# Turning weights in place between two chains, instead of turning, storing and loading them back

## The chip, the cores, the metric

One core of one Trainium2 chip. The metric is the device time of one execution in microseconds (us), as a median of several.

The chain of the kernel works in order of time, so most readings are lengths of stages, from one landmark to the next. Six batches of runs were made, and the kernel before has medians from 3148 to 3178 us over them. Every run is therefore compared with the runs of the kernel before in its own batch.

## The reference, cut to what matters

A memory-augmented recurrent attention over 64 segments of 32 rows, with 8 memory rows in front, 32 heads of 128, model width 512; and beside it a dense layer with squared ReLU. Asked for are the output and all gradients.

```python
mem = mem0
for s in range(n_seg):                                  # 64 steps, each needs mem of the last
    h = jnp.concatenate([mem, xs[s]], axis=1)           # 8 + 32 rows of 512
    q, k, v = (jnp.einsum('btd,dhe->bhte', h, W) for W in (Wq, Wk, Wv))
    p = _softmax(jnp.where(mask, jnp.einsum('bhqe,bhke->bhqk', q, k) * scale, -1e9))
    o = jnp.einsum('bhte,hed->btd', jnp.einsum('bhqk,bhke->bhqe', p, v), Wo)
    mem = o[:, :M, :].copy()
# out = x + A(layernorm(x)) + B(layernorm(x)); returned: out and the vjp with grad_out
```

The backward pass needs each weight with its two inner axes exchanged ("turned"): the forward projections contract over the model width, the backward ones over the head's columns.

## The kernel before: the parts that the argument touches

PE is TensorE, DVE VectorE, ACT ScalarE, POOL GpSimd; PEld are TensorE's weight loads, SPq is the Sync queue. Names that begin with S_ are tensors in DRAM. vM holds the values of a block's memory rows, loaded back from S_A, into which f_N, the projections of a step, are stored. dN are the projections of the rows that do not feed the recurrence (the left rows); OT, OC and OCl are attention outputs on their way to DRAM, OTL and ON those of the left rows; gol is their incoming gradient. A gather is a product with Wo (in the backward chain with another turned weight) that brings the heads back to the model width. The seam is the stretch between the last forward projection and the first product of the left rows. A weight is 4 MB in bf16. The forward chain plays 16 blocks of 4 steps in a fixed order for each engine. In each step the kernel turned 128 x 1024 elements: eight transposes on PE (`wt`), a copy from PSUM to SBUF on DVE (`we`), a store of 256 KB on the Sync queue (`ws`):

```python
def wt():
    ps["wt"] = fr.tile([P, 8 * P], BF16, name="ps_wt", tag="r")
    for n in range(8):
        ...                                             # x = a 128 x 128 block of Wo, Wv, Wk or Wq
        transpose_to(ps["wt"][:, n * P:(n + 1) * P], x)
def we():
    st["wt"] = fo.tile([P, 8 * P], BF16, name="wtt", tag="wtt")      # one buffer
    ENGS["we"](st["wt"][:], ps["wt"][:])
def ws():
    dma(S_WOT[...] if t == 3 else S_WT[...], st["wt"][:]...)         # Sync queue
# ... and the eviction of other rows shares that buffer:
    st["dN", i // 2] = fo.tile([P, GW], BF16, name="dN", tag="wtt")
```

At the end of the chain a load on the GpSimd queue brings turned Wo back to where Wq and Wk were; the others come in twelve loads of 1 MB, one in each iteration of the next stage (the "left rows": the work of the backward pass that doesn't depend on the recurrence, mixed with products for the dense layer's weight gradients, which read `wA` and `wB`):

```python
def load_back():
    wq_cm.__exit__(None, None, None); wk_cm.__exit__(None, None, None)
    ...
    back["WoT"] = bw.tile([P, DC, HD], BF16, name="WoT")
    pdma(back["WoT"][:], S_WOT[:])
# left rows:
def chunk(b, eng=dma):
    ...
    side[b > 0] = wg.tile([P, TC, D], BF16, name="wA", tag="wA", bufs=1)
    eng(side[b > 0][:], ...)                            # wA, 2 MB
    part[b] = wg.tile([P, TC, CH], BF16, name="wB", tag="wB")
    eng(part[b][:], ...)                                # wB, 1 MB
o["first"] = lambda: (load(i_, nc.scalar), chunk(i_, pdma))
...
    for t, h in pieces[i_:i_ + 1]:
        pdma(WT[t][:, h:h + 8, :], S_WT[:, t, h:h + 8, :])
```

## Time and profile before

| | us |
|---|---|
| median of the first three runs | 3175.75 (3164.9 to 3184.37) |
| profiled span | 3166.7 |
| forward chain, first to last forward projection | 917.2 |
| from there to the last left gather of the forward pass | 30.6 |
| from there to the first product of the left rows (wA, wB) | 52.7 |
| left rows, from there to the first backward projection | 228.9 |
| backward chain, first to last backward projection | 963.6 |

A row of groups gives busy time and mean duration; a wait gives its total, how often, and the longest; a timeline row gives start, duration and in brackets the idle time before it and what ended it.

### The profile page before, as it was taken

The page shows a single profiled execution, that of the slowest core. Times are in us where ns is not written, and L with a number is a line of the kernel's source. Part 1 is how long each engine was busy: PE and PEld are TensorE (multiplying, and loading weights), DVE is VectorE, ACT ScalarE, POOL GpSimd, SP SyncE. Part 2 cuts the span into 40 slices and gives each one's busy share as a digit, 9 for nine tenths or more (in the row PEclk, how much of TensorE's full clock was granted, in tenths as well). Part 3 has the DMA queues.
Part 4 walks back from the last instruction along what each step waited for, and adds up shares of the span by engine and source line. Part 5 has one row for each costly group of instructions (what it writes and reads, how often), then busy time and mean ns, then how long its engine had stood idle before and what let it go on. Part 6 is the DMA issues. An engine that isn't in the chain of part 4 may idle for free.

```text
span 3166.7 us, 115555 instructions
## 1 busy us (share of the span) xinstructions
PE 2726.4 (86%) x51672; PEld 1404.3 (44%) x51672; DVE 1261.0 (40%) x3515; ACT 1012.6 (32%) x2356; POOL 384.3 (12%) x702
## 2 busy tenths in 40 slices
PE   8996899999999885478789888888888649999998
PEld 4453455555554442235444444444444324444443
DVE  5442555555565563232444444444444301100101
ACT  2322444444454442122333333333333201111111
POOL 0000000000000000122222222222222100000000
PEclk9998999999999997789999999999999879999999
DMA  9557476666767767999577677767766799999993
GB/s 265 163 183 210 123 196 186 183 181 190 190 170 191 181 175 196 233 290 263 142 185 173 162 188 172 170 172 183 172 162 188 176 229 193 220 184 217 183 186 85
DMA packets 842563, 594.40 MB, mean 188 GB/s; under 512 B 595745, under 2 KB 726578, under 8 KB 837074
## 3 DMA queue, kind: packets, MB, share of 16 engines
q1 hardware_dynamic: 814850, 489.73, 65.0%
q0 software_dynamic: 25584, 96.10, 9.8%
q8 instruction: 405, 6.64, 0.9%
q10 hardware_dynamic: 1632, 1.18, 0.1%
q14 instruction: 92, 0.75, 0.1%
HBM read 205.14 MB, written 250.10 MB: 144 GB/s over the span
## 4 chain that ended last, share of the span: by engine, by line
PE 29%; SPq 9%; ACT 4%; DMA 3%; issue 3%; DVE 2%; ACTq 0%; POOLq 0%; POOL 0%; DVEq 0%
PE ps_gR L431 9%; PE ps_gw L1471 8%; SPq L1396 6%; PE b_pp L518 4%; PE ps_proj L390 3%; DMA out_dram<-wt 2%; PE ps_RL L1168 2%; PE ps_sum L440 2%; ACT gk L374 1%; ACT gON L374 1%; ACT gv L374 1%; SPq L1382 1%; DMA gn<-S_ON 1%; ACT R L374 1%; SPq L1399 1%
## 5 line engine op out<-in xcount | busy, mean ns | idle before, releaser
L1471 PE MATMUL ps_gw<-gn,HNc 128*128 128x512 bf16 x1920 | 418.5, 380 | 8.5 <-ACT wt L1446 8.5
L1471 PEld LDWEIGHTS <-HNc 128*128 128x128 bf16 x1920 | 188.3, 98 | 234.1 <-issue 11.5
L374 ACT CAST f_N<-ps_proj 128x512 bf16<-128x512 f32 x384 | 218.1, 587 | 193.5 <-PE ps_proj L390 155.5
L1446 ACT CAST wt<-ps_gw 128x512 bf16<-128x512 f32 x126 | 69.2, 592 | 560.3 <-DMA out_dram<-wt 361.6
L390 PEld LDWEIGHTS <-X 128*32 128x32 bf16 x6144 | 160.3, 99 | 175.8 <-issue 22.7
L1429 DVE TENSOR_TENSOR gx<-ps_rows,gb 128x512 f32<-128x512 f32 x16 | 11.1, 692 | 423.0 <-PE ps_rows L1427 392.4
L1471 PE MATMUL ps_gw<-GOc,gn 128*128 128x512 bf16 x640 | 142.6, 386 | 28.1 <-DMA gn<-S_ON 28.1
L431 PE MATMUL ps_gR<-WT,gv 128*32 128x512 bf16 x2048 | 150.8, 388 | 11.3 <-ACT gOT L374 4.2
L431 PE MATMUL ps_gR<-WT,gk 128*32 128x512 bf16 x2048 | 142.4, 395 | 9.8 <-ACT gk L374 6.6
L390 PE MATMUL ps_proj<-Wk,X 128*32 128x512 bf16 x2048 | 137.9, 403 | 8.2 <-DVE X L915 4.0
L431 PE MATMUL ps_gR<-WT,gq 128*32 128x512 bf16 x2048 | 140.4, 397 | 3.9 <-issue 3.9
L390 PE MATMUL ps_proj<-Wq,X 128*32 128x512 bf16 x2048 | 134.5, 394 | 6.6 <-DVE X L453 6.5
L374 ACT CAST gON<-ps_proj 128x512 bf16<-128x512 f32 x128 | 75.0, 586 | 165.5 <-PE ps_proj L390 160.2
L390 PE MATMUL ps_proj<-WoT,GT 128*32 128x512 bf16 x2048 | 123.6, 383 | 4.5 <-POOL GT L1198 3.3
L829 POOL COPY kM<-f_kT 128x256 bf16<-128x256 bf16 x64 | 25.8, 402 | 831.9 <-DVE f_kT L377 831.9
L431 PE MATMUL ps_R<-Wo,OT 128*32 128x512 bf16 x2048 | 122.6, 380 | 1.2 <-DVE OT L377 1.2
L440 PE MATMUL ps_sum<-identF,R 128*128 128x128 f32 x512 | 102.1, 300 | 25.0 <-ACT R L374 16.1
L390 PE MATMUL ps_proj<-Wv,X 128*32 128x512 bf16 x2048 | 121.6, 378 | 0.0
L1471 PEld LDWEIGHTS <-gn 128*128 128x128 bf16 x640 | 63.5, 99 | 105.9 <-DMA gn<-S_ON 28.4
L374 ACT CAST gk<-b_pp 128x256 bf16<-128x256 f32 x192 | 65.9, 381 | 138.7 <-PE b_pp L518 132.3
L440 PEld LDWEIGHTS ps_sum<-identF,R 128*128 128x128 f32 x512 | 56.9, 145 | 86.3 <-ACT R L374 58.9
L377 DVE COPY R<-ps_gR 128x256 f32<-128x256 f32 x64 | 27.2, 425 | 157.6 <-ACT R L374 116.0
(241 smaller groups left out, 4886.4 us busy)
## 6 DMA issues: line engine op xcount, KB each, us to landing
S_A<-f_N SPq DMA_DIRECT2D x64, 512.0 KB
S_A<-f_N SPq DMA_DIRECT2D x64, 256.0 KB
S_GB<-gv SPq DMA_DIRECT2D x32, 512.0 KB
S_GB<-gq SPq DMA_DIRECT2D x32, 512.0 KB
S_GB<-gk SPq DMA_DIRECT2D x32, 512.0 KB
gn<-S_ON SPq DMA_DIRECT2D x16, 1024.0 KB
out_dram<-wt SPq DMA_DIRECT2D x128, 128.0 KB
b_kN<-S_A POOLq DMA_DIRECT2D x63, 256.0 KB, 4.1
```

What stands on the lines that cost most here:

```text
L374: nc.scalar.copy(out, in_)
L377: nc.vector.tensor_copy(out, in_)
L390: nc.tensor.matmul(ps[32 * g:32 * g + 32, :], lhsT=hT[:, dc, :], rhs=W[:, dc, c:c + 4 * P], start=(dc == 0), stop=(dc == DC - 1), tile_pos ...
L431: nc.tensor.matmul(R[32 * g:32 * g + 32, :], lhsT=XT(k, g), rhs=W[:, g * KH + k, :], start=(first and k == 4 * h), stop=(last and k == 4 * ...
L440: nc.tensor.transpose(st["T"][:, c * P:(c + 1) * P], R4()[:, c * P:(c + 1) * P], identF[:])
L518: nc.tensor.matmul(o, lhsT=N_[32 * g:32 * g + m, kk * P:(kk + 1) * P], rhs=X(kk)[32 * g:32 * g + m], start=(i == 0), stop=(i == len(jobs) ...
L1168: nc.tensor.matmul(ps["R", i][32 * g:32 * g + 32, :], lhsT=B_[n][:, k, g, :], rhs=W[:, g * KH + k, :], start=(ps["n", i] == 1 and m == 0), ...
L1382: nc.sync.dma_start_transpose(t_[:, 0:NB, dc * P:(dc + 1) * P], srcT[:, dc, :])
L1396: nc.sync.dma_start_transpose(t_[:, b, :].rearrange("p (k e) -> p k e", k=KH), blocks(b)[:, g].rearrange("p k r -> p (k r)"))
L1399: dma(t_[32 * j:32 * j + 32, NB:RC_ALL, :], left_(g).rearrange("(c j) r x -> j r c x", j=SPB)[j])
L1446: nc.any.tensor_copy(wt[:], ps[:])
L1471: nc.tensor.matmul(ps[:], lhsT=l(rc), rhs=r(rc), start=(n == 0), stop=(n == RC_ALL - 1))
```

## The change

Intent: the weights have the same size turned as unturned, so each 128 x 1024 block can be turned where it lies: eight transposes into PSUM and one copy back over the block. Nothing is stored or loaded, and no turning runs inside the forward chain: 18 turns of Wk and Wq and 16 of Wo run in its tail, 30 more (the rest of Wq, and Wv) in the iterations of the left rows. The price: turned in place, a weight is read as four runs of 128 columns with gaps.

```diff
-    S_WT = dram.tile([P, 3, H, D], BF16, name="S_WT")
-    S_WOT = dram.tile([P, DC, HD], BF16, name="S_WOT")
...
+    def turned_columns(W):
+        return lambda dc, c: W[:, c // P:c // P + 4, dc * P:(dc + 1) * P]
+    def turned_heads(W):
+        return lambda h: W[:, :, h * P:(h + 1) * P]
+    def turn_weight(ps, W, n, ev):
+        x = W[:].rearrange("p a b -> p (a b)")[:, n * 8 * P:(n + 1) * 8 * P]
+        for i in range(8):
+            transpose_to(ps[:, i * P:(i + 1) * P], x[:, i * P:(i + 1) * P])
+        ev(x, ps[:])
... (weight_turn with wt, we, ws, and all their places in the order: removed)
-            pdma(back["WoT"][:], S_WOT[:])
+        TURNS = [(Wqkv[t], n) for t in (1, 0, 2) for n in range(HD * DC // (8 * P))]
+        TURNS_O = [(Wo, n) for n in range(HD * DC // (8 * P))]
+            after = {"ob0": 2, "ob1": 2, "L.tu1": 10, "L.ob1": 2, "L.G1": 1, "L.G0": 1}
+            after_o = {"L.ra": 6, "L.tb": 5, "L.xt": 5}
... (left rows:)
-                for t, h in pieces[i_:i_ + 1]:
-                    pdma(WT[t][:, h:h + 8, :], S_WT[:, t, h:h + 8, :])
+                def T_(i=i):
+                    if TURNS:
+                        turn_weight(lr.tile([P, 8 * P], BF16, name="ps_wt", tag="r"), *TURNS.pop(0), (acp, vcp)[i])
... (projections and gathers read through columns, heads_of, turned_columns, turned_heads;
     the buffers of the left rows are laid out anew, as the weights keep their places)
```

## The prediction

> **What bounds the kernel now.** I read the busy slices of the page first, then the busy times by stage, then the waits, then the order of time at the seams. The stages are known from which tiles run when: forward chain 308 to 1215 us, its tail to 1253, start of the left-rows stage to 1303, that stage to 1532, backward chain to 2512, weight gradients to the end.
>
> ```profile
> PE   8996899999999885478789888888888649999998
> ...
> DMA  9557476666767767999577677767766799999993
> ...
> 308.00:1215.00 907.00, 838.63 (x18799) 450.33 (x18800) 531.90 (x1567) 422.49 (x934) 51.23 (x127) 0.98 0.66 178
> ...
> 1253.00:1303.00 50.00, 4.40 (x108) 2.42 (x108) 4.96 (x12) 2.15 (x4) 2.66 (x5) 0.55 0.96 212
> 1303.00:1532.00 229.00, 175.07 (x3276) 106.53 (x3278) 71.55 (x166) 59.56 (x138) 52.84 (x100) 0.92 0.96 257
> ```
>
> The columns of a stage are PE, PEld, DVE, ACT and POOL busy, granted clock, DMA share, GB/s. The forward chain has PE busy 838.6 of 907 us (92%) and the DMA engines 66%: PE and the recurrence bound it. From 1253 to 1532 it is the reverse: DMA share 0.96, PE idle 45.6 of 50 and 53.9 of 229 us. That is where DMA traffic has a price.
>
> In the forward chain I looked for what the turning costs there. Its PE part is small (eight transposes at 57 ns from start to start, 0.45 us a step), its DVE copy 0.68 us a step:
>
> ```profile
> L165 PE MATMUL ps_wt<-ident,Wv x128: 219/219/230, 530.4 to 743.5; 128*128 128x128 bf16 x128
> L377 DVE COPY wtt<-ps_wt x64: 651/682/693, 312.8 to 1207.4; 128x1024 bf16<-128x1024 bf16 x64
> ...
> SPq L796 <- DVE wtt L377: 85.3, 35, 7.0
> ...
> PE f_pp L518 <- DMA vM<-S_A: 21.2, 28, 1.5
> ...
> 998.14 0.40 SPq L899 DMA_DIRECT2D S_A<-E  x1
> 1002.04 0.32 SPq L796 DMA_DIRECT2D S_WT<-wtt  x1
> 1002.41 1.33 SPq L678 DMA_TRANSPOSE OC<-OT  x1
> 1003.79 2.84 SPq L537 DMA_DIRECT2D f_vLs<-S_NL  x8
> 1006.68 2.82 SPq L532 DMA_DIRECT2D vM<-S_A  x4
> ```
>
> A wait shows total us, times, longest. The Sync queue issues in order, and 35 times it stands still for the copy that fills wtt, 85.3 us in all between 320 and 1190. In the block at 998 it idles from 998.54 to 1002.04, and all that stands behind it, last the four loads of vM, goes out that much later. PE then waits for vM in the product that needs it, 21.2 us in 28 waits, some 1.4 us in each of 15 blocks.
>
> At the seam one transfer stands in the way:
>
> ```profile
> 1214.49 0.56 POOL L912 DMA_DIRECT2D WoT<-S_WOT  x1 [9.60 <-PE ps_proj L390]
> 1215.04 0.33 SPq L680 DMA_DIRECT2D S_ON<-OC  x1
> 1230.73 1.49 SPq L678 DMA_TRANSPOSE OC<-OT  x1
> ...
> 1241.22 0.20 PE L518 MATMUL f_pp<-ETL,vM 32*128 32x32 bf16 x1 [13.43 <-DMA vM<-S_A]
> ```
>
> The 4 MB load of WoT starts at 1214.5 and lands 16.0 us later; the 256 KB store issued behind it at 1215.04 is what the next line of the Sync queue waits for, until 1230.73 (15.3 us of wait). In the steady chain the same wait is 2.5 us at the longest. PE idles 13.43 us for it.
>
> In the left-rows stage an iteration starts with its projection:
>
> ```profile
> 1320.16 1.91 PE L390 MATMUL ps_proj<-WoT,gol 128*32 128x512 bf16 x32
> 1332.54 1.91 PE L390 MATMUL ps_proj<-WoT,gol 128*32 128x512 bf16 x32
> 1348.96 1.91 PE L390 MATMUL ps_proj<-WoT,gol 128*32 128x512 bf16 x32
> 1361.67 1.91 PE L390 MATMUL ps_proj<-WoT,gol 128*32 128x512 bf16 x32
> 1381.69 1.91 PE L390 MATMUL ps_proj<-WoT,gol 128*32 128x512 bf16 x32
> ```
>
> Undisturbed, an iteration takes 12.4 us (1320.16 to 1332.54) and PE has almost no gap in it. The others are stretched, to 16.4, 20.0, later 19.2, 16.9 and 21.0 us. Summed over the stage the excess is some 33 us (4.0 + 7.6 + 1 + 6.8 + 4.5 + 8.6, and small change).
>
> **What the Trainium skill says.** "DMA: Bandwidth & Descriptors", section "Issuing engines are not separate DMA queues", says that transfers issued from any engine run on the same 16 DMA engines and interleave. The seam agrees: a load from the GpSimd queue holds up a store of the Sync queue for 15.3 us. "TensorE: Matmul & The Clock Gate", section "Step-by-step: what each phase is for", says of a matmul's throughput that it is "purely `N cycles`": nothing in it names the spacing of the moving columns. This matters because the turned weights are now read as four runs of 128 columns. The trace before has a test: the mask product with 160 moving columns reads four runs of 40 out of rows of 64, the one with 256 columns reads them without gaps.
>
> ```profile
> L406 PE MATMUL ps_sc<-maskA,ident x128: 229/233/243, 309.0 to 1217.7; 128*128 128x160 bf16 x128
> L406 PE MATMUL ps_scL<-maskL,ident x32: 272/278/283, 355.4 to 1225.3; 128*128 128x256 bf16 x32
> ```
>
> The same page, section "Single matmul latency", gives (398 + N)/2.4 ns at full clock: 232.5 for 160 and 272.5 for 256. Measured 233 and 278: the gaps cost nothing. No row has a gap as wide as the 8 KB of the turned Q, K and V.
>
> **The change part by part.**
> (1) Forward chain. Removed: 64 turns (512 transposes, 29 us of PE; 64 copies, 43.6 us of DVE), 64 stores of 256 KB and their issues. Not much of the 29 us is on the path: in the steps that I followed the transposes stand where PE would wait (at 615.74 until 616.19, with ET ready at 616.28), at 627.24 they cost 0.12 us, at 654.13 some 0.2; mean about 0.08, times 64 makes 5 us. Eviction of dN shares the buffer of wtt and waits for its stores 54 us on ACT in all (43.2 and 10.8), mostly where ACT would idle: at 622.38 it cost 0.3 us. Some 28 waits by 0.1 make 3. The wait for vM is on the path, as the transposes that feed the next step stand behind it in PE's order: with the queue freed by 2 to 3 us, more than the mean stall of 1.4, I take 17 of the 21.2 us. Sum: 25 us less.
> (2) Seam. WoT is not loaded: the store lands some 3 us after its issue instead of 15.7, and vM and all behind it come 12 us earlier. Added: 34 turns, of Wk, two of Wq, and Wo. Each costs PE 0.45 us, and a copy: on DVE 0.68 us (row of wtt), on ACT an estimated 1.1 us (a 128x512 copy takes 0.59). ACT and DVE alternate, so two turns take some 1.1 us. Fourteen lie before the product that waits for vM, in idle time. Sixteen, of Wo, come after its last reading, 8 x 1.1 = 9 us ahead of the first left projection; but PE is idle 45.6 us there and the loads set the end. Net 11 us less.
> (3) Left-rows stage. Twelve loads of 1 MB go. The software queue moved 34.06 MB in 32.5% of the 317 us from 1215 to 1532, 3.0 us of all 16 engines a MB: 38 us of DMA work. From 1303 to 1532 the DMA was busy 0.96 x 229 = 220 us; without them 182. PE's own need is 229 - 33 = 196, and 30 turns add 30 x 0.45 = 13.5, as in this order they stand where PE is already busy: 209. So PE becomes the bound, at a DMA load of some 87%. I leave 7 us of the stalls: 216, that is 13 us less.
> (4) Backward chain: the same matmuls with other access patterns, 0. The first buffers of the weight gradients lie where weights are read to the end: 1 us more.
> Sum: -25 - 11 - 13 + 1 = -48; 3175.75 - 48 = 3128 us.
>
> **Rivals.**
> Strided reading slows PE: 2048 projections and 7680 gathers and left products in the backward chain, four at a time in the array. If each run of 128 cost 5 ns more, 9728 / 4 x 20 ns = 49 us would eat the whole gain. The mask rows speak against it. I give it 5%.
> PE filler: if the turns only filled waits and the vM stall gets another releaser (the store of OC, the loads of f_vLs ahead of it in the queue), the forward chain gives 8 instead of 25, and the whole 3145. For it: SP issues back to back from 1002 to 1009.5. Against: it stood idle 3.5 us just before.
> Seam: the loads that start the left-rows stage now lie on other forward tiles, as Wo keeps its place. The first product waited 19.70 us for its operand wB, whose load had waited for the stores of OCl at 1294. If these buffers come free earlier, up to 20 us more are won (3108); if the larger wA now waits for the same late tiles, the seam gains nothing (3139).
> Left-rows stage stays DMA-bound: a stall is set by a single load's queueing, and turns and stalls add up. Then this stage is even, 3141. Or, with PE's waits absorbing the turns, it gives 26, 3115.
>
> **Range and chances.** The terms move on their own: forward 8 to 35 less, seam 0 to 30 less, left rows 0 to 26 less, the rest 0 to 10 more. Their extremes rarely meet; in eight of ten cases I expect 3098 to 3158 around 3128. A gain of 2% is 3112 or below, for which the seam's buffers or the forward chain must give more than I take: 0.24. Slower by 2% needs slow strided reading and more: 0.03. Within 2%: 0.73.
>
> **What would show it.** (1) holds if the Sync queue's waits for wtt are gone, PE's for vM fall to under 5 us, and the forward chain takes some 882 us. (2) holds if the last vM wait of PE is under 3 us and the first product of the left-rows stage starts 60 to 80 us after the end of the chain's last forward projections, against 83 (1219.9 to 1302.84). (3) holds if its iterations come near 13.3 us and its DMA share falls to about 0.87. (4) holds if gathers keep their 379 ns and the backward chain its 980 us; a longer one is the first rival. If the stalls in (3) stay, or the forward chain is hardly shorter, I am wrong in the direction of 3145 to 3160.

## More of the kernel before

One more view of the kernel before is needed later: the busy time of each engine in windows of 2 us, here around the wait for vM in the block at 604 us. The columns are PE, PEld, DVE, ACT, POOL busy, then the granted TensorE clock, the DMA share and GB/s.

```profile
604.00:606.00 2.00, 0.80 (x33) 0.68 (x34) 0.14 (x1) 0.31 (x1) 0.00 (x0) 1.00 1.03 370
606.00:608.00 2.00, 1.95 (x44) 1.36 (x45) 1.25 (x4) 1.07 (x2) 0.00 (x0) 0.51 1.03 399
608.00:610.00 2.00, 2.00 (x28) 0.82 (x24) 0.72 (x2) 0.34 (x1) 0.00 (x0) 0.64 0.89 334
```

PE is busy for 0.80 of the first 2 us; then it is busy all the time, but at half clock.

## The result, and the profile after

The changed kernel took 3083.14 us (3073.23 to 3088.68, 4 runs) against 3178.04 (3164.9 to 3184.37, 4 runs): a ratio of 0.970, with an interval of 0.966 to 0.975. A ratio is the mean time of one kernel's runs over that of the other's of the same rounds, so not quite the ratio of the medians. Two later batches gave 0.976 (0.973 to 0.980) and 0.976 (0.973 to 0.979). So it is faster by 2.4 to 3.0%, 75 to 95 us, where 48 us had been forecast and 3098 was the lower end of the range. All outputs are right.

In the profiles (3166.7 and 3086.9 us, 79.8 less) the time went here; the third column has the terms of the forecast:

| stage | before | after | difference | forecast |
|---|---|---|---|---|
| start to first forward projection | 302.3 | 300.5 | -1.8 | 0 |
| forward chain | 917.2 | 870.5 | -46.7 | -25 |
| seam, first part: to the last left gather | 30.6 | 20.5 | -10.1 | -11 with the next |
| seam, second part: to the first product of the left rows | 52.7 | 37.9 | -14.8 | |
| left rows, to the first backward projection | 228.9 | 223.2 | -5.7 | -13 |
| backward chain | 963.6 | 968.4 | +4.8 | 0 |
| the rest | 671.4 | 665.9 | -5.5 | +1 |

The last two rows are within what the backward chain (958 to 979 us) and the rest (657 to 672 us) differ from one profile to another. Three others vary too: in runs of the kernel before with edits elsewhere (e1, e4 and g4 below), the first part of the seam took 25.2 to 29.5 us, the second 51.4 and 55.1 (e1, e4), and the left rows 224.4 and 241.1 (e4, e1). In the runs that keep the left rows of the changed kernel, these took 220.7 to 223.2.

The stages after, with the columns as above:

```profile
306.00:1166.00 860.00, 793.29 (x18300) 415.42 (x18296) 493.94 (x1503) 423.04 (x934) 50.74 (x126) 0.99 0.65 168
...
1229.50:1452.50 223.00, 184.60 (x3504) 119.15 (x3504) 83.76 (x186) 73.80 (x152) 47.81 (x91) 0.95 0.81 219
```

The chain's PE share is as before (92%), in 47 us less. In the left rows the DMA share fell from 0.96 to 0.81 and PE rose from 175 to 185 us; v3 below tests whether PE is the bound now.

The waits after, of the Sync queue and of PE, 320 to 1190 us:

```profile
SPq L707 <- DMA S_ON<-OC: 83.7, 45, 3.2
...
PE f_pp L545 <- DMA vM<-S_A: 2.8, 6, 0.8
```

The 85.3 us for wtt are gone, and the queue now waits most for the store of OC (83.7 us, before 37.5), but PE's wait for vM fell from 21.2 to 2.8 us. The seam after, on the Sync queue:

```profile
1172.51 0.67 SPq L709 DMA_DIRECT2D S_ON<-OC  x1
...
1176.62 1.24 SPq L707 DMA_TRANSPOSE OC<-OT  x1
1177.95 3.54 SPq L559 DMA_DIRECT2D vM<-S_A  x4
```

From the issue of the store to the next transpose it is 4.1 us, where it was 15.7; and the projections of the left rows come every 13.94 us or within 0.06 us of it, except for three of the fourteen stretches after the first (18.4, 10.5 and 17.6 us):

```profile
1236.04 1.91 PE L390 MATMUL ps_proj<-Wo,gol 128*32 128x512 bf16 x32
1249.98 1.91 PE L390 MATMUL ps_proj<-Wo,gol 128*32 128x512 bf16 x32
```

The gathers of the backward chain after, now with gaps in the moving operand, keep their median; before they had 376/379/634:

```profile
L458 PE MATMUL ps_gR<-Wq,gq x2048: 376/379/634, 1461.6 to 2430.2; 128*32 128x512 bf16 x187
```

### The profile page after: what moved, and what is told of

Same layout as the page of the kernel before. It is cut to its first block, busy times and chain, and to the rows that moved or that the text cites. A ratio compares the mean times of both kernels' runs of the same rounds, so it can differ in the third digit from the quotient of the medians.

```text
span 3086.9 us, 115454 instructions
## 1 busy us (share of the span) xinstructions
PE 2706.9 (88%) x51672; PEld 1396.2 (45%) x51672; DVE 1243.1 (40%) x3481; ACT 1046.3 (34%) x2390; POOL 378.0 (12%) x689
## 4 chain that ended last, share of the span: by engine, by line
PE 36%; SPq 5%; ACT 4%; issue 3%; DVE 3%; DMA 2%; ACTq 0%; POOLq 0%; POOL 0%; DVEq 0%
PE ps_gw L1460 13%; PE ps_gR L458 10%; PE b_pp L545 4%; PE ps_proj L390 4%; SPq L1385 3%; PE ps_sum L467 2%; PE ps_RL L1156 2%; ACT gk L372 1%; ACT gON L372 1%; ACT gv L372 1%; SPq L1371 1%; DMA out_dram<-wt 1%; ACT R L372 1%; PE ps_sc L435 1%; DVE gq L375 1%
## 5 line engine op out<-in xcount | busy, mean ns | idle before, releaser
L458 PE MATMUL ps_gR<-Wv,gv 128*32 128x512 bf16 x2048 | 148.4, 382 | 10.5 <-ACT gOT L372 4.6
L458 PE MATMUL ps_gR<-Wk,gk 128*32 128x512 bf16 x2048 | 146.4, 406 | 10.7 <-ACT gk L372 5.7
L458 PE MATMUL ps_gR<-Wq,gq 128*32 128x512 bf16 x2048 | 142.8, 402 | 4.3 <-issue 4.2
L390 PE MATMUL ps_proj<-Wk,X 128*32 128x512 bf16 x2048 | 130.1, 384 | 6.4 <-DVE X L909 4.5
L390 PE MATMUL ps_proj<-Wo,GT 128*32 128x512 bf16 x2048 | 123.9, 384 | 4.4 <-POOL GT L1186 3.3
L467 PE MATMUL ps_sum<-identF,R 128*128 128x128 f32 x512 | 99.4, 293 | 31.4 <-ACT R L372 24.4
```

The lines of the kernel that those rows point to most:

```text
L390: nc.tensor.matmul(o, lhsT=hT[:, dc, :], rhs=x, start=(dc == 0), stop=(dc == DC - 1), tile_position=(0, 32 * g))
L458: nc.tensor.matmul(o, lhsT=XT(k, g), rhs=x, start=(first and k == 4 * h), stop=(last and k == 4 * h + 3), tile_position=(0, 32 * g))
L467: nc.tensor.transpose(st["T"][:, c * P:(c + 1) * P], R4()[:, c * P:(c + 1) * P], identF[:])
```

## The experiments

Two questions: why the chain gained 47 and not 25, and why the seam gained a second part while the left rows gained less than half. The measure for the chain is the changed kernel's, 867.6 us (mean of its profiles with 870.5, 867.6 and 864.6). "Half-clock time" is the time between 320 and 1160 us in which the granted clock was 0.5, summed from windows of 1 us: 41.0 us in the kernel before, 6.8, 6.8 and 3.4 us in the three profiles of the changed one. (Up to 1190 us the kernel before has 12 stretches; the expectations of e1 and e4 say 14.) Each chain below is read from one profile; those of the changed kernel differ by 6 us.

### The chain: which part of the old work costs?

**e1_store_from_act.** The kernel before with one of four stores of wtt, the one that stands ahead of the loads of vM, issued from ACT, so that the Sync queue need not wait for it.

```diff
-                dma(S_WOT[...] if t == 3 else S_WT[...],
+                (nc.scalar.dma_start if n2 % 4 == 0 and n2 else dma)(S_WOT[...] if t == 3 else S_WT[...],
```

> The kernel before, except that every fourth of its 64 stores of turned weights (the one that stands ahead of the loads of vM in the Sync queue) is issued from ACT. All transposes, copies and stores stay. Theory A (the Sync queue stands still for the copy, vM comes late, PE waits, and the idle PE then runs 3.4 us at half clock): the waits for vM fall from 21 us to under 6, the half-clock stretches between 320 and 1190 us from 14 to at most 4, and the forward chain gets 30 to 45 us shorter. Theory B (the work of the turns on PE and DVE is what the chain paid for): 0 to 10 us shorter. My prediction's own term would give 17 us.

3171.59 us, ratio 0.997 (0.995 to 0.9995). The queue's waits for wtt fell from 79.3 us in 34 waits (320 to 1160) to 28.5 in 20, and no wait of PE for vM was left. But the chain fell only to 904.0, as another wait grew: DVE stood 21.6 us (3.4 before) for the store of the last wtt to free the one buffer. Inconclusive as a test of the wait alone: it put another in its place.

**e2_work_only** and **e3_wait_only.** The changed kernel, once with the transposes and copies of old in the chain but no store; once with only a small copy on DVE and a small store that waits for it, at the old places of `we` and `ws`.

```diff
 e2: +  (wt and we as before, in their old places)
     +            def ws():
     +                pass
 e3: +            def we():
     +                st["wt"] = fo.tile([P, 128], BF16, name="tiny", tag="tiny")
     +                nc.vector.tensor_copy(st["wt"][:], ident[:])
     +            def ws():
     +                dma(S_TINY[n2], st["wt"][:])
```

> The changed kernel, with the transposes and copies of the kernel before put back into its forward chain, without the stores (their result is not used; outputs stay right). Theory A: the forward chain gets at most 10 us longer, as this work lies in waits and nothing waits for a store. Theory B (work): 25 to 45 us longer, as in the kernel before.

> The changed kernel, with a small copy on DVE (128x128) and a small store of it (32 KB) where the copy and the store of a turned weight stood, so that the Sync queue waits for DVE at the same places, with hardly any work or traffic. Theory A: vM comes late again, the waits for it return (10 to 21 us), 8 to 14 half-clock stretches return, and the chain gets 20 to 40 us longer. Theory B: under 5 us longer.

e2: 3096.44 us, ratio 0.974 (0.972 to 0.976), chain 871.7 (+4.1), half-clock time 6.8 us. e3: 3105.09 us, ratio 0.978 (0.975 to 0.981), chain 886.1 (+18.5); PE waits 16.4 us for vM in 24 waits, the queue 92.7 us for the small copy; half-clock time 10.2 us. The work alone is nearly free, as forecast (5). The wait alone costs what the forecast gave it (17). Together that is 23 of 50.

**e4_filler_before_vM.** The kernel before, with 40 useless transposes of a constant on PE just ahead of the product that waits for vM.

```diff
+                    if p == 0 and 0 < b < NB - 1:
+                        fill = fr.tile([P, 8 * P], BF16, name="ps_fill", tag="r")
+                        for n in range(40):
+                            transpose_to(fill[:, (n % 8) * P:(n % 8 + 1) * P], ident[:])
```

> The kernel before, with 40 transposes of the identity (some 2.3 us of PE) ahead of the product that waits for vM, in each block but the first and last. They shorten no wait for a transfer. Theory A with its second half (half clock after idle PE): the half-clock stretches between 320 and 1190 fall from 14 to at most 4, and the chain gets 5 to 20 us shorter although PE has 32 us more work. Theory A without the clock (only the wait costs): the chain gets as long as before or up to 20 us longer, as the filler overruns the waits.

3175.22 us, ratio 0.999 (0.997 to 1.001). The filler takes the place of the wait (0.3 us of it are left), and half-clock time fell from 41.0 to 17.1 us, five stretches, where at most four had been expected. In blocks 1 to 10, the step with the wait took 15.85 us instead of 15.73, and the step after it 13.39 instead of 14.28; the chain fell by 7.0 us to 910.2. So work that is of no use makes the next step shorter by 0.9 us a block: the half clock after the wait costs time. Over the whole kernel the difference is not resolved.

**f1_traffic_only** and **f2_whole_old_chain.** The changed kernel with stores of 256 KB from a tile that nobody writes, at the old places; and with the whole old turning put back into the chain (its result unused).

```diff
 f1: +            def we():
     +                pass
     +            def ws():
     +                dma(S_W64[n2], Wqkv[2][:, 0, 0:8 * P])
 f2: +  (wt, we and ws as before, S_WT and S_WOT written and not read)
```

> The changed kernel with 64 stores of 256 KB in its forward chain, at the places of the stores of before, from a weight tile that is always there: traffic and issue time, but no wait for DVE, no turning, no buffer shared with dN. So far: the work alone cost the chain 1.2 us, the wait alone 15.6, of the 46.7 that the chain gained. Theory A2 (the rest is the wait together with what follows from it, half clock): traffic alone costs under 6 us. Theory C (the stores' 16 MB slow the other transfers that the chain waits for): 12 to 30 us, with waits for vM or for the buffer of f_N in the trace.

> The changed kernel with all that the forward chain of before did for the turning (transposes, copies, stores of 256 KB, the buffer shared with dN), the result unused. This must close the sum: the chain 40 to 50 us longer than in the changed kernel, 9 to 14 half-clock stretches between 320 and 1160 us, vM waits near 20 us. If it comes out under 30, the chain's gain has another source than the turning.

f1: 3072.85 us, ratio 0.975 (0.971 to 0.978), chain 868.8 (+1.2). f2: 3126.33 us, ratio 0.990 (0.987 to 0.994), chain 916.1 (+48.5), half-clock time 47.8 us. The whole difference of the chains is thus in the turning; but its parts alone give 4.1 + 18.5 + 1.2 = 24. The rest belongs to combinations.

**f4_no_shared_buffer, f3_wait_and_traffic, f5_wait_and_work.** The changed kernel with wait, work and traffic, but a store that reads another tile, so that the buffer shared with dN is never held; then the wait with one companion each.

```diff
 f4: +  (wt; we as before, and behind it a small copy)
     +            def ws():
     +                dma(S_TINY[n2], st["tiny"][:])
     +                dma(S_W64[n2], Wqkv[2][:, 0, 0:8 * P])
 f3: +  (e3, and behind its small store)  dma(S_W64[n2], Wqkv[2][:, 0, 0:8 * P])
 f5: +  (f4 without the store of S_W64)
```

> The changed kernel with the turning work of the old one (transposes and copies), with the wait of the Sync queue (a small store that waits for a small copy behind the large copy) and with stores of 256 KB, but these read a tile that nobody writes, so the tile that is turned into, and which dN shares, is never held by a store. The whole old chain put back gave 45.6 us. Theory 1 (the stalled PE and the clock that follows make the rest): the half-clock stretches return (10 or more of 3.4 us between 320 and 1160), and the forward chain is 35 to 48 us longer than in the changed kernel. Theory 2 (dN's waits for the large store in the one shared buffer make the rest): it is 14 to 25 us longer, as with the small store alone (15.6), and the half-clock stretches stay at 2 to 5.

> The changed kernel with the small copy and the small store that waits for it, and behind it in the Sync queue a store of 256 KB from a tile that nobody writes: the wait and the traffic together, without the transposes and the large copies. The wait alone made the forward chain 15.6 us longer, the traffic alone 1.7 us shorter, work, wait and traffic together without a shared buffer 46 to 49 us longer. If wait and traffic together are what costs (vM's loads start late and then queue behind the large store): the chain is 35 us or more longer, with PE's waits for vM over 20 us. If the traffic adds nothing: 13 to 20 us.

> The changed kernel with the transposes and copies of the turning and with the wait of the Sync queue (small store behind the copies), but without the stores of 256 KB. If wait and work together are what costs (the real copy waits for PE's transposes and stands behind other work, so the queue is held later and longer than by the small copy alone): the forward chain is 35 us or more longer than the changed kernel's, with half-clock stretches of 25 us or more. If the work adds nothing to the wait: 13 to 20 us.

f4: 3131.78 us, ratio 0.995 (0.991 to 0.998). f3: 3116.31, 0.987 (0.984 to 0.991). f5: 3117.56, 0.988 (0.984 to 0.992). The chains:

| wait of the queue | work | traffic | buffer held by the store | chain, us | against 867.6 | half clock, us | PE waits for vM, us |
|---|---|---|---|---|---|---|---|
| - | - | - | - | 867.6 | | 3.4 to 6.8 | 0.8 to 2.8 |
| - | yes | - | - (e2) | 871.7 | +4.1 | 6.8 | 2.8 |
| - | - | yes | - (f1) | 868.8 | +1.2 | 6.8 | 0.4 |
| yes | - | - | - (e3) | 886.1 | +18.5 | 10.2 | 16.4 |
| yes | - | yes | - (f3) | 901.6 | +34.0 | 13.7 | 19.9 |
| yes | yes | - | - (f5) | 907.5 | +39.9 | 41.0 | 19.5 |
| yes | yes | yes | - (f4) | 917.1 | +49.5 | 30.7 | 24.4 |
| yes | yes | yes | yes (f2) | 916.1 | +48.5 | 47.8 | 17.9 |

The buffer shared with dN costs nothing that shows (f4 against f2; f4 has a small copy and a small store more), though ACT waits for it in f2. The wait is what makes the rest dear: behind it the traffic costs 15.5 us instead of 1.2, and the work 21.4 instead of 4.1. The half-clock stretches of f4 were fewer than theory 1 expected (8, not 10) and its chain a little longer (49.5, not up to 48); f3 just missed the 35 and the 20 us that were to show its point, with 34.0 and 19.9; f5 met its own.

The two companions act differently. With the work, PE's clock falls after most of the waits; the windows of f5 (columns as above):

```profile
596.00:598.00 2.00, 1.92 (x51) 1.12 (x53) 1.82 (x5) 0.00 (x0) 0.00 (x0) 0.79 1.04 409
598.00:600.00 2.00, 2.00 (x24) 0.75 (x20) 0.14 (x1) 0.58 (x1) 0.00 (x0) 0.50 1.01 363
```

The wait alone (e3) has 10.2 us at half clock, f5 41.0: 30.8 us more, which are at most 15.4 us lost, if all of it was work on the path; the work's excess there is 21.4. So the clock can't be all of it. With the traffic the clock stays (13.7 us), but ACT, which evicts the projections into f_N, waits for the store of the last f_N. The waits of ACT in f3:

```profile
ACT f_N L372 <- DMA S_A<-f_N: 57.4, 16, 4.8
```

against 10.0 us in 3 waits with the wait alone and 14.1 in 5 with the traffic alone. In the kernel before both are there, on other rows:

```profile
ACT dN L374 <- DMA S_WT<-wtt: 43.2, 22, 3.3
ACT f_N L374 <- DMA S_A<-f_N: 23.1, 9, 4.4
```

That these two are the way in which the combinations cost is an argument from what appears along with them; only e4 touches the clock by itself, and no run took the f_N wait away alone.

Nor is it shown why the clock falls in some blocks only. PE waits for vM in some 13 blocks between 320 and 1160 in e3, f3 and f5 alike, 16.4, 19.9 and 19.5 us, yet there are 3, 4 and 11 stretches at half clock. In the clock record of each of these runs, and of the kernel before, the stretches begin at whole multiples of 3.413 us from one another; the 11 of the kernel before follow steps of that grid in which PE was busy 1.1 to 2.1 of 3.4 us. So where a wait falls on the grid may count as much as the work that goes with it, and no run moved the waits alone.

### The seam and the left rows

**e5_wgrad_buffers_low.** The changed kernel, with the buffers of wA and wB allocated first, so that they lie on those tiles of the chain on which they lay before. It asks whether the place of the buffers makes the second part of the seam.

```diff
-    with sb("la", 2) as la, sb("ls", 2) as ls, sb("lo", 1) as lo_, sb("wg", 2) as wg,
+    with sb("wg", 2) as wg, sb("la", 2) as la, sb("ls", 2) as ls, sb("lo", 1) as lo_,
```

> The changed kernel, with the buffers of the weight-gradient operands (wA, wB) put at the bottom of the stage's space, where they lie on the forward tiles that they lay on before (X, kL, N, OT), instead of higher up. Theory A (the seam gained some 15 us because wB no longer waits for the last stores of OCl): from the last forward gather to the first weight-gradient product 10 us and more longer than the 37.9 of the changed kernel, with a wait of the GpSimd queue for OCl. Theory B (it gained because 4 MB of WoT no longer come in): within 4 us of 37.9.

3080.03 us, ratio 0.976 (0.972 to 0.979). From the last left gather to the first product 37.3 us, as in the changed kernel (37.9). wA now went out at 1183, before the gather, and the gol of the projections late instead. I took this as support for the other theory, that the 4 MB of WoT were missed there. The next three runs took that back.

**g1_loads_as_traffic.** The changed kernel with the old loads as copies from DRAM to DRAM that nobody waits for.

```diff
+                        pdma(S_D0[:], A_Wv.rearrange("(c p) h e -> p c (h e)", p=P))      # for WoT
+                if i_ < 12:
+                    pdma(S_D1[i_], A_Wk[:, 8 * (i_ % 4):8 * (i_ % 4) + 8, :]...)            # left rows
```

> The changed kernel with the loads of the old one put back as plain traffic from DRAM to DRAM, which no engine waits for: 4 MB on the GpSimd queue at the place of the load of WoT, and 1 MB in each of the first twelve iterations of the left rows. If the traffic is what cost the time: the last forward projection to the last left gather is 28 to 31 us (20 in the changed kernel), the left gather to the first weight-gradient product 48 to 54 (37.9), and the left rows 235 to 255 us, since their stalls return on top of the turns (223.2). If it was the buffers or the order of the queues: each within 4 us of the changed kernel.

3110.39 us, ratio 0.988 (0.984 to 0.992). The seam did not move (20.3 and 36.4 us), but the run does not test its first part: the 4 MB waited for nothing and went out at 1147, 20 us before the last projection. The left rows did move: 236.7 us, 15 more than the 221.2 of the same batch, with the DMA share back at 0.96. So the twelve loads cost the left rows some 15 us, also beside the turns.

**g3_load_in_its_place** and **g4_wA_behind_wB.** The changed kernel with a 4 MB load that waits for the last projections as the old one did (Wq loaded once more over itself, and turned last); and the kernel before with one line moved: the first wA goes out behind wB.

```diff
 g3: -        TURNS = [(Wqkv[t], n) for t in (1, 0, 2) ...
     +        TURNS = [(Wqkv[t], n) for t in (1, 2, 0) ...
     +                        pdma(Wqkv[0][:], A_Wq.rearrange("(c p) h e -> p c (h e)", p=P))
 g4: -                eng(side[b > 0][:], ...)          # wA, at the start of the left rows; now under "if b:"
              eng(part[b][:], ...)                       # wB
     +            if b == 0:
     +                eng(side[False][:], ...)
```

> The changed kernel with a load of 4 MB on the GpSimd queue that waits, like that of WoT in the old kernel, for the last reading of the forward projections: Wq is loaded once more with its own contents (Wq is turned last for this, after Wk and Wv). The earlier attempt had put its 4 MB out 20 us before the last projection, so it did not test this place. If the load in its place cost the seam its first part: the last forward projection to the last left gather takes 28 to 32 us (20 to 21 in the changed kernel). If the arrival of the 4 MB cost the second part too: last left gather to first weight-gradient product 48 to 54 us; if the second part has another cause: 36 to 41, as in the changed kernel.

> The old kernel with one edit: at the start of the left rows, the 2 MB load of wA is issued behind the load of wB instead of ahead of it, so it goes out after the tail's stores of OCl, as it does in the changed kernel, instead of into the tail's small transfers at 1247. Theory C (in the old kernel this early load crowds out the tail's transposes and stores; in the changed one it happens to wait for a buffer): last left gather to first weight-gradient product falls from 52.7 us to 34 to 42. Theory B (the 4 MB of WoT and their delay are what cost there): it stays at 50 to 56. The seam before the last left gather is unchanged (30.6) under both.

g3: 3082.32 us, ratio 0.976 (0.972 to 0.980). The load went out 5.0 us before the start of the last projection matmul, as of old. First part of the seam 26.4 us, a little under what was expected, so it gave back 6 of the 10 (all, if measured by e1, e4 and g4, which have the old load there and took 29.5, 25.2 and 26.7); the transpose behind the store was issued 9.8 us after it (4.1 without the load, 15.7 before). Second part 35.4: the load has no share in that.

g4: 3152.91 us, ratio 1.000 (0.995 to 1.005), but inside it much moved. First the kernel before, the rows of its Sync and GpSimd queues after the last left gather (1250.1):

```profile
1247.23 1.46 SPq L749 DMA_TRANSPOSE ON<-OTL  x1
...
1268.64 0.32 SPq L755 DMA_DIRECT2D S_OL<-ON  x1
...
1245.63 0.54 POOL L956 DMA_DIRECT2D gol<-S_GLT  x1 [27.45 <-DMA S_ON<-OC]
1247.65 1.17 POOL L1036 DMA_DIRECT2D wA<-in_grad_out_dram  x1 [1.48 <-ACT OTL L374]
```

wA goes out half a microsecond behind the small transpose of ON, and the store of ON, which waits for it, can be issued only 21 us later. With wA moved, the same rows in g4 (last left gather 1245.3):

```profile
1242.45 1.54 SPq L749 DMA_TRANSPOSE ON<-OTL  x1
...
1246.81 0.32 SPq L755 DMA_DIRECT2D S_OL<-ON  x1
...
1274.69 0.53 POOL L1040 DMA_DIRECT2D wB<-S_AN  x1 [33.33 <-DMA S_VTM<-vTM]
1275.22 1.17 POOL L1042 DMA_DIRECT2D wA<-in_grad_out_dram  x1
```

4 us instead of 21 (in e1 and e4, with the early wA, 19 and 11). The last store of the tail (the fourth of OCl) came 26.6 us after the gather instead of 41.9. The first product came 43.8 us after it instead of 52.7, just outside what Theory C expected, and far from B: 8.9 of the tail's 15.3 arrive there, as wA itself is now what is waited for (27.1 us). The first part of the seam, expected unchanged, took 26.7 us instead of 30.6. And the left rows took 236.0 us instead of 228.9 (224.4 to 241.1 without this edit), so the whole is even. In the changed kernel, too, wA goes out only behind the tail, without anybody having asked for it, as wA's new place lies on tiles that the tail reads last:

```profile
1211.45 1.17 POOL L1024 DMA_DIRECT2D wA<-in_grad_out_dram  x1 [30.69 <-DMA OCl<-OT]
```

There the last store of OCl is issued 19.0 us after the gather, and nothing of the old loads follows wA. So 8.9 of the 14.8 us of the second part of the seam are shown to come from the early load of wA in the tail; the remaining 6 us (43.8 against 37.9) are open. So is why the early wA of e5 cost its tail so little (22.4 us to the last store of OCl): there gol was not on the way at the same time, but no run separates that.

**v1_turns_in_first_wait, v2_half_turns_in_first_wait.** The changed kernel with 30, or 15, of the turns of the left rows put behind the first projections of the stage, to run in the wait for the first loads, copied by DVE alone; v2 keeps one turn in each iteration.

```diff
+                    if b == 0 and nm == "o1mm":
+                        while TURNS:                     # v2: for _ in range(15)
+                            turn_weight(lr.tile([P, 8 * P], BF16, name="ps_wt", tag="r"), *TURNS.pop(0), vcp)
```

> The changed kernel, with the 30 turns of the left-rows stage taken out of its 15 iterations and done at once, copied by DVE alone, after the first left projection, where PE now idles some 22 us for loads. The iterations of the changed kernel take 13.93 us where 12.38 is what they took undisturbed before: turns of 0.9 us of PE and a wait of 0.5 us for a PSUM buffer behind the first of them. If that reading is right: iterations of 12.4 us again, the stage from its first weight-gradient product to the backward chain 15 to 23 us shorter, the first product at most 4 us later; in all 12 to 20 us faster than the changed kernel. If DMA is what bounds the iterations (rival), under 6 us.

> The changed kernel with 15 of the 30 turns of the left rows done in the idle time of the first iteration, copied by DVE, and one turn an iteration kept, the second one. 15 turns take some 10.5 us of DVE, which lie inside the wait of 27.8 us, so the first weight-gradient product comes at most 4 us later. Left rows: 223.2 less 15 x 0.8 = 12 us, to 209 to 214. The whole 6 to 12 us faster than the changed kernel on the same chip. If the first product is again 10 us or more later, the copies hold up what stands behind them on DVE and the gain is lost.

v1: 3075.41 us, ratio 0.974 (0.970 to 0.978). v2: 3075.51, ratio 0.977 (0.974 to 0.980), beside the changed kernel itself with 3074.55 and 0.976 (0.973 to 0.980) on the same chip. No gain. The left rows did get shorter, v1's to 200.8 us with iterations of 12.4 us again, as expected, and v2's to 208.4; but the first product came 51.6 and 43.5 us after the last left gather instead of some 37.5. The timeline of PE in v2 says why:

```profile
1198.80 1.91 PE L390 MATMUL ps_proj<-Wo,gol 128*32 128x512 bf16 x32
1200.64 1.07 PE L163 MATMUL ps_wt<-ident,Wq 128*128 128x128 bf16 x16
1222.13 7.50 PE L163 MATMUL ps_wt<-ident,Wq 128*128 128x128 bf16 x96 [20.42 <-ACT l_gON L372]
```

Two turns ran in the wait. The stage has four PSUM buffers; the two projections ahead hold two of them until ACT evicts them (l_gON), and ACT's own queue stands in the loads until 1221. The other turns came after the wait instead of in it.

> The changed kernel once more, on the chip of the three that follow, as their measure; against the kernel before a ratio of 0.970 to 0.977 as on the first chip, and stages within 3 us of its first profile (forward chain 870.5, last left gather to first weight-gradient product 37.9, left rows 223.2).

**v3_turns_before_projections.** So 28 turns ahead of the projections.

```diff
+                    if b == 0 and nm == "o0mm":
+                        for _ in range(28):
+                            turn_weight(lr.tile([P, 8 * P], BF16, name="ps_wt", tag="r"), *TURNS.pop(0), vcp)
```

> The changed kernel with 28 of the 30 turns of the left rows done ahead of the first projections of that stage, copied by DVE. In the two earlier attempts only two turns ran in the wait, as the projections ahead of them held PSUM buffers until ACT came to evict them. Ahead of the projections all four buffers are free: 28 turns by 0.70 us of DVE are 19.6 us, from 1198 to 1218, while the loads end at 1218 to 1224. First left-rows projection about 20 us later, but the first weight-gradient product at most 3 us later than in the changed kernel (last left gather to it 37 to 41 us); from there to the last projection 183 to 188 us (206 to 208). The whole 15 to 22 us faster than the changed kernel: a ratio of 0.968 to 0.971 to the kernel before, if the changed kernel has 0.975. If the turning is not what fills the left rows, the stretch stays over 200.

> The changed kernel once more as the measure of the run beside it, on its chip: ratio to the kernel before 0.970 to 0.977.

```profile
1199.10 7.53 PE L163 MATMUL ps_wt<-ident,Wq 128*128 128x128 bf16 x110
1206.62 8.38 PE L163 MATMUL ps_wt<-ident,Wv 128*128 128x128 bf16 x112
1214.99 1.91 PE L390 MATMUL ps_proj<-Wo,gol 128*32 128x512 bf16 x32
...
1225.00 5.37 PE L1035 MATMUL ps_w<-wA,wB 128*128 128x512 bf16 x16
```

Now they fill the wait: the first product comes 35.9 us after the last left gather (38.2 in the run of the changed kernel beside it), and from there to the last left projection it is 187.4 us instead of 208.0. So the 28 turns cost the left rows 20.6 us, 0.74 us each, on PE's path. The whole took 3065.0 us (3057.16 to 3067.49, 5 runs), ratio 0.972 (0.969 to 0.975), against 3072.88 and 0.976 (0.973 to 0.979) for the changed kernel in the same rounds. That is the fastest of all versions by the median, by 8 us, where 15 to 22 were expected; the two intervals touch. In its profile the backward chain was 974.5 us against 958.4 beside it, with 71.6 us of half clock in the stretch from 1430 to 2420 against 44.4. Other kernels with the same backward code show 960.7 to 979.2 us, so it may be chance; whether the earlier start shifts that chain to a worse place is open.

## Why the prediction was wrong

The direction was right and every sign of the large terms, and several of the signs that it named came out: no waits for wtt, PE's wait for vM 2.8 us (under 5) and none at the seam (under 3), gathers at 379 ns, a backward chain of its old length. Others missed: the chain took 870.5 us (882), the first product of the left rows came 58.0 us after the end of the last forward projection (60 to 80), the iterations 13.94 us (13.3), with a DMA share of 0.81 (0.87). Its rivals of slow strided reading and of mere filler both fell. The size was wrong: 80 us by the profiles instead of 48.

- **Forward chain, the step that failed.** The forecast added 5 for PE's transposes, 3 for dN and 17 for the wait for vM, to 25. Each of the first and last is right when it stands alone (4.1 and 18.5), and dN is nothing. But the terms do not add: the wait with the work costs 40, with the traffic 34, with both 49.5. That is the step that failed: the sum left out what the terms cost together. Of what the forecast missed, e4 shows the half clock behind the wait, 0.9 us a block; that the rest is more of it and the late stores of f_N, for which ACT waits, is argued from the traces and not shown. The clock was to be seen: in the windows before, 41 us at 0.5, in 11 stretches, and the one shown lies right behind the wait. The Trainium skill has it in "TensorE: Matmul & The Clock Gate", section "HAM oscillation — how this bites in real kernels": waits for data that re-throttle the PE, again and again. The trace agrees in kind, with shorter waits than the 3 to 5 us there (1.24 and 0.46 us before the stretch shown). The forecast used two other sections of that page.
- **Seam, first part.** "12 us earlier" was about right (10.1; 5 to 9 against e1, e4 and g4), by the cause named for at least 6 of them (g3).
- **Seam, second part.** The forecast let it stand at 0 net. Its rival named other buffers: if they came free *earlier*, up to 20 us more; if wA waited for the late tiles, no gain. The second of these happened, and the seam still gained 14.8: as the buffer of wA came free *later*, its load left the tail alone (8.9 of the 14.8 by g4). That a gain came here at all owes nothing to the forecast.
- **Left rows.** The loads: their stalls fell from 33 us to some 5 (v3's stage of 202.5 us, less its two turns of 1.5, over PE's need of 196), where 7 was taken; g1 brings only 15 us back, beside the turns. The mis-sized term is the turning: 30 turns by 0.45 us of PE make 13.5, but each cost 0.74 (v3): some 22 us. In the iteration from 1236 us the two turns take 0.62 and 0.54 us of PE, and the product behind the first waits another 0.55 us for DVE; before, the same product had no wait. By these profiles that cut the gain from 13 to 5.7; but the old stage alone varies from 224.4 to 241.1 us, so the gain itself is anything from 1 to 20.
- **Range.** The extremes of three terms were given, and the forward term's own upper end (35) was below what came (46.7). A term that holds a stall of the TensorE should have had room upwards for the clock.

## What to carry to other kernels

Work that hides in idle time is not free if a queue waits for it: here the same transposes and copies cost 4 us without the wait and 21 with it, so look first for the in-order queue that stands still for a small producer, and expect more than the stall itself when it goes. Read the granted clock in windows of 1 or 2 us right behind each recurring stall of PE, not the mean of the stage (0.98 before). And a buffer that comes free late can be a gain where its load would meet a tail of small dependent transfers; an order of two loads is worth trying by itself.

## What the Trainium skill lacked or had wrong

- "TensorE: Matmul & The Clock Gate", section "HAM oscillation — how this bites in real kernels", gives as the rule that PE must have no idle gaps over some 3.4 us. Here two waits of 1.24 and 0.46 us in a window with 0.80 of 2 us busy were followed by some 3.4 us at a clock of 0.5, and there were 11 such stretches between 320 and 1160. (Its next section does say that frequent short idles make the clock oscillate.)
- The same page, section "Part 4: PE-mode transpose", says that the full clock does not engage for transposes. In v3, nothing but transposes (222 of them recorded) ran on PE from 1199.1 to 1215.0, and the clock was 1.00 in the windows of 4 us from 1202 to 1214. It gives 275 to 390 ns for one of 128 x 128; here the median is 219 ns, and 57 ns from start to start.
- No page says what gaps between long runs of a moving operand cost ("Advanced Engine Details and Errata", section "SBUF Cachelines", is about steps from access to access). Here, runs of 128 columns with gaps of up to 8 KB cost nothing: 379 ns before and after for 128 x 512.
- "DMA: Bandwidth & Descriptors", section "Issuing engines are not separate DMA queues", says that all transfers interleave, but not what that does to a chain of small ones: with a 2 MB load half a microsecond behind, the store that waits for a transpose was issued 21 us after it instead of 4 (19 and 11 us in e1 and e4).
